# Moving q, k, v preparation beside the first-layer MLP stage and running attention two batches ahead, in a fused attention and MLP kernel

## Chip, cores, metric

One core of one Trainium2 chip. The metric is the device time of one execution in microseconds (us); medians of several runs are quoted, and ratios where two kernels are compared. The trace of one profiled execution per kernel is what the readings rest on; its span lies about 2 us below the time of the same execution.

## The reference, cut to what matters

Batch, heads, sequence and head size are 8, 8, 576 and 64. Model and hidden sizes are 512 and 2048. Inputs and outputs are float32.

```python
scores = scale * q @ k^T + (cum[i] - cum[j])     # cum: running sum of log f
attn   = softmax(causal(scores));  o = attn @ v
x      = o as (B*S, H*D)                          # 4608 tokens of 512
out    = gelu_tanh(x @ w_in) @ w_out              # 512 -> 2048 -> 512
```

## The kernel before

Work goes by groups `i` of four heads, two groups per batch. For one group an *attention step* makes scores (TensorE), exponentials (ScalarE), the causal mask (VectorE), and the product with v for the group before (TensorE). That product carries the row sums along: v is extended by a column of weights. The sums then go through DRAM, for one pair of heads at a time: two small DMAs collect them (`den`), VectorE inverts them, one DMA stores them (`rrow`), two DMAs bring them back broadcast over 64 partitions (`rb`), and POOL multiplies (`scale_out`, writing `xT`, the input of the MLP). I call this the *row-sum chain*.

```python
def step(i, j, old, n, fill, per_round, qk_loads=(), v_loads=()):
    for x in qk_loads: load_qk(x)          # 8 DMAs on the sync queue
    for x in v_loads:  load_v(x)           # 5 DMAs on the sync queue, 256-byte pieces
    for r in range(4):
        if i is not None: score_round(i, r)
        if j is not None: attn_out(j, r); den_load(j, r)
        if r == 0 and n is not None: cast_k(n); cast_q(n)              # POOL
        if r == 1:
            if old is not None: den_spread(old, 1); scale_out(old, 0)  # rrow, rb; POOL
            if n is not None: transpose_k(n)                           # VectorE
        if r == 2:
            if n is not None: transpose_q(n)
            if i is not None: make_vaug(i)                             # POOL
        if i is not None and r > 0: mask(i, r - 1)
        pull(fill, per_round)              # second-layer matmuls fill the gaps
        if r == 3:
            if j is not None: den_spread(j, 0)
            if i is not None: mask(i, 3)
            if old is not None: scale_out(old, 1)                      # last multiply
# ... cut ...
    step(0, None, None, 1, none, 0); step(1, 0, None, None, none, 0)
    for c in range(4): load_w_out(c)       # POOL queue, casts on the way
    step(None, 1, 0, 2, none, 0, qk_loads=[2, 3], v_loads=[2]); finish_out(1)
    for ft in range(N_FT): mlp_in(0, ft)   # first first-layer stage
    fill = mlp_out(out_tiles(0)); pull(fill, 24)
    attention(1, fill, 3); attention(2, fill, 2)
    # ... cut: rest of fill ...
    for ft in range(N_FT): mlp_in(1, ft)   # second first-layer stage
    for b in range(3, B):
        fill = mlp_out(out_tiles(b - 2))
        attention(b, fill, 9)              # two steps, each loading q, k of i+2 and v of i+1
        # ... cut: rest of fill ...
        for ft in range(N_FT): mlp_in(b - 1, ft)
```

`mlp_in(b, ...)` is the *first-layer stage* of a batch, 128 matmuls of 288 columns. It needs all of `xT` of that batch, so only its first six matmuls can run before the last `scale_out`; where it "starts" or "gets going" below is after that wait. The order of instructions is set by hand, and the sync queue issues its DMAs in that order: in the timeline below, a store whose data were ready at 345.4 us is issued at 353.1, after the loads ahead of it.

The softmax here doesn't subtract the row's maximum and nothing guards it: scores larger than these inputs give would overflow.

Of the kernel before, what the change touches and what calls it, by code (L numbers as in the profile page):

```python
# [8 lines left out]
FP32 = mybir.dt.float32  # L9
# [7 lines left out]
def kernel(  # L17
# [10 lines left out]
    nc = tc.nc  # L28
# [32 lines left out]
    singles = ctx.enter_context(tc.tile_pool(name="singles", bufs=1))  # L61
    ostage_pool = ctx.enter_context(tc.tile_pool(name="ostage", bufs=3))
    den_pool = ctx.enter_context(tc.tile_pool(name="den", bufs=3))
    rb_pool = ctx.enter_context(tc.tile_pool(name="rb", bufs=4))
    dram_pool = ctx.enter_context(
        tc.tile_pool(name="scratch", bufs=4, space=bass.MemoryType.DRAM))
    psS = ctx.enter_context(tc.tile_pool(name="psS", bufs=2, space=bass.MemoryType.PSUM))
# [3 lines left out]
    def many(n, shape, dtype, name):  # L71
        return [singles.tile(shape, dtype, name=f"{name}{i}") for i in range(n)]
# [7 lines left out]
    k_nat = many(2, [128, NA, 2, D], FP32, "k_nat")  # L80
    q_bf = singles.tile([128, NA, 2, D], BF16, name="q_bf")
    k_bf = singles.tile([128, NA, 2, D], BF16, name="k_bf")
    v_nat = many(2, [128, NT, 4, D], FP32, "v_nat")
    qT = many(2, [128, S, 2], BF16, "qT")
    kT = many(2, [128, SPAD, 2], BF16, "kT")
    v_aug = many(2, [128, NT, 4, 128], BF16, "v_aug")
# [9 lines left out]
    shift = singles.tile([128, 1], FP32, name="shift")  # L96


    def load_qk(i):
        b, h0 = i // QPB, 4 * (i % QPB)  # L100
        for src, dst in ((k, k_nat[i % 2]), (q, q_nat[i % 2])):

            for h in range(4):
                nc.sync.dma_start(  # L104
                    out=dst[32 * h:32 * h + 32].rearrange("p a e d -> p a (e d)"),
                    in_=src[b, h0 + h].rearrange("(a p e) d -> p a (e d)", p=32, e=2),
                )

    def load_v(i):
        b, h0 = i // QPB, 4 * (i % QPB)  # L110
        for t in range(NT):
            n = min(128, S - 128 * t)
            nc.sync.dma_start(  # L113
                out=v_nat[i % 2][:n, t, :, :],
                in_=v[b, h0:h0 + 4, 128 * t:128 * t + n, :].rearrange("h p d -> p h d"),
            )

    w_in_hbm = moe_w_in.rearrange("(t p) n -> p t n", p=128)
# [22 lines left out]
    def cast_k(i):  # L141
        nc.gpsimd.tensor_copy(k_bf, k_nat[i % 2])

    def cast_q(i):
        nc.gpsimd.tensor_copy(q_bf, q_nat[i % 2])

    def transpose_k(i):
        transpose_one(k_bf, kT[i % 2])

    def transpose_q(i):  # L150
        transpose_one(q_bf, qT[i % 2])

    def make_vaug(i):
        va = v_aug[i % 2].rearrange("p t (x y) c -> p (t x) (y c)", y=2)
        va = va.rearrange("p m (e c) -> p m e c", c=64)
        vn = v_nat[i % 2].rearrange("p t (x y) d -> p (t x) y d", y=2)
        w = wT[:, i, :, :].rearrange("p t (x y) -> p (t x) y", y=2)
        nc.gpsimd.tensor_mul(va[:, :, 0:4:3, :], vn,
                             w.unsqueeze(3).to_broadcast([128, 2 * NT, 2, D]))
        nc.gpsimd.tensor_copy(va[:, :, 1:3, 0:1], w.unsqueeze(3))  # L160

    def score_round(i, r):
# [109 lines left out]
    def out_tiles(b):  # L272
        n0 = 9 * (b // 2)
        return range(n0, n0 + 4) if b % 2 == 0 else range(n0 + 4, n0 + 9)


    def setup():
        nc.sync.dma_start(out=f_sb, in_=f.rearrange("b h s -> (b h) s"))
        for i in range(2):
            load_qk(i)  # L280
            load_v(i)
        make_identity(nc, ident_f32)
        make_upper_triangular(nc, utri_f32, val=1.0, diag=True)
        for t_ in v_nat:
            nc.gpsimd.memset(t_[64:128, NT - 1, :, :], 0.0)
        for t_ in v_aug:
            nc.gpsimd.memset(t_, 0.0)
        cast_k(0)
        cast_q(0)
        for c in range(4):  # L290
            load_w_in(c)

        nc.vector.memset(ones_f32, 1.0)
        nc.vector.memset(wT[64:128, :, NT - 1, :], 0.0)
        nc.vector.memset(shift, -64.0)
        for t_ in kT:
            nc.vector.memset(t_[:, S:SPAD, :], 0.0)
        nc.vector.tensor_scalar(f_sb, f_sb, 1e-4, 1.0, op0=ALU.max, op1=ALU.min)
        nc.scalar.activation(f_sb, f_sb, AF.Ln)
        nc.vector.tensor_copy(utri[:, 0, :], utri_f32)  # L300
        ps_lt = psM.tile([128, NT * BH], FP32, name="ps_lt", tag="m")
        for t in range(NT):
            jw = min(128, S - 128 * t)
            nc.tensor.transpose(ps_lt[:jw, t * BH:(t + 1) * BH],
                                f_sb[:, 128 * t:128 * t + jw], ident_f32)
        nc.vector.tensor_copy(logfT[:, :(NT - 1) * BH], ps_lt[:, :(NT - 1) * BH])
        nc.vector.tensor_copy(logfT[:LAST, (NT - 1) * BH:], ps_lt[:LAST, (NT - 1) * BH:])
        cum_ps = psM.tile([128, NT * BH], FP32, name="cum_ps", tag="m")
        for t in range(NT):
            jw = min(128, S - 128 * t)  # L310
            for tp in range(t + 1):
                jp = min(128, S - 128 * tp)
                lhsT = utri_f32[:jp, :jw] if tp == t else ones_f32[:jp, :jw]
                nc.tensor.matmul(cum_ps[:jw, t * BH:(t + 1) * BH], lhsT,
                                 logfT[:jp, tp * BH:(tp + 1) * BH],
                                 start=(tp == 0), stop=(tp == t))
        for (rows, t0, t1) in ((128, 0, NT - 1), (LAST, NT - 1, NT)):
            nc.scalar.activation(
                wT[:rows, :, t0:t1, :].rearrange("p i t h -> p t i h"),
                cum_ps[:rows, t0 * BH:t1 * BH].rearrange("p (t i h) -> p t i h", i=NQ, h=4),  # L320
                AF.Exp, scale=-1.0, bias=shift[:rows, :])
        transpose_k(0)
        transpose_q(0)


    def pull(it, n):
# [1 line left out]
            if next(it, False) is False:  # L328
                return

    def step(i, j, old, n, fill, per_round, qk_loads=(), v_loads=()):


        for x in qk_loads:
            load_qk(x)
        for x in v_loads:
            load_v(x)
        for r in range(4):
            if i is not None:
                score_round(i, r)  # L340
            if j is not None:
                attn_out(j, r)
                den_load(j, r)
            if r == 0:
                if n is not None:
                    cast_k(n)
                    cast_q(n)
            if r == 1:
                if old is not None:
                    den_spread(old, 1)  # L350
                    scale_out(old, 0)
                if n is not None:
                    transpose_k(n)
            if r == 2:
                if n is not None:
                    transpose_q(n)
                if i is not None:
                    make_vaug(i)
            if i is not None and r > 0:
                mask(i, r - 1)  # L360
            pull(fill, per_round)
            if r == 3:
                if j is not None:
                    den_spread(j, 0)
                if i is not None:
                    mask(i, 3)
                if old is not None:
                    scale_out(old, 1)

    def finish_out(j):  # L370
        den_spread(j, 1)
        scale_out(j, 0)
        scale_out(j, 1)

    none = iter(())

    def attention(b, fill, per_round):
        for i in range(b * QPB, b * QPB + QPB):
            step(i, i - 1 if i > 2 else None, i - 2 if i > 3 else None,
                 i + 1 if i + 1 < NQ else None, fill, per_round,  # L380
                 qk_loads=[i + 2] if i + 2 < NQ else [],
                 v_loads=[i + 1] if i + 1 < NQ else [])

    with tc.manual_schedule():
        setup()
        step(0, None, None, 1, none, 0)
        step(1, 0, None, None, none, 0)
        for c in range(4):
            load_w_out(c)
        step(None, 1, 0, 2, none, 0, qk_loads=[2, 3], v_loads=[2])  # L390
        finish_out(1)
        for ft in range(N_FT):
            mlp_in(0, ft)
        fill = mlp_out(out_tiles(0))
        pull(fill, 24)
        attention(1, fill, 3)
        attention(2, fill, 2)
        for x in fill:
            pass
        for ft in range(N_FT):  # L400
            mlp_in(1, ft)
        for b in range(3, B):
            fill = mlp_out(out_tiles(b - 2))
            attention(b, fill, 9)
            if b == B - 1:
                step(None, NQ - 1, NQ - 2, None, none, 0)
                finish_out(NQ - 1)
            for x in fill:
                pass
            for ft in range(N_FT):  # L410
                mlp_in(b - 1, ft)
        fill = mlp_out(out_tiles(B - 2))
        for ft in range(N_FT):
            mlp_in(B - 1, ft)
            pull(fill, 4)
        for x in fill:
            pass
        for x in mlp_out(out_tiles(B - 1)):
            pass
# [30 lines left out]
```

## Time and profile before

| | before |
|---|---|
| time, median | 485.4 us |
| span of the profiled run | 481.7 us |
| TensorE busy | 366.5 us, 76% |
| first first-layer stage runs without a break from | 76.2 us |
| second first-layer stage starts at | 156.1 us |
| one batch of the steady part (mean of four) | 51.2 us |
| from the seventh first-layer stage to the end | 66.5 us |

The page's first two parts of the kernel before: busy time (PE is TensorE's matmuls, PEld its weight loads, DVE VectorE, ACT ScalarE), and the span in 40 slices of 12 us (busy tenths of TensorE, its granted clock in tenths, that is the share of full clock that the profile records as granted, and the busy tenths of the DMA engines).

```profile
PE 366.5 (76%) x2818; PEld 218.0 (45%) x2851; DVE 147.9 (31%) x253; ACT 204.2 (42%) x274; POOL 182.3 (38%) x148
...
PE   4462107988570999789975999699929997999996
...
PEclk9997556999876999989997999899989999799999
DMA  9969920098955804781286318461643022200111
```

TensorE has the most work, and each notch in its row is idle time. The DMA row stands at 6 to 9 tenths in the first five slices and is high again in spells of every batch later. (This trace has 2818 of the program's 2851 matmuls on record, so its busy time of TensorE is slightly low.)

Stretches of the kernel before, cut where each first-layer stage gets going: length, busy time of PE, PEld, DVE, ACT and POOL, granted clock, DMA share, GB/s. The DMA share adds up the times of the packets and can read above 1.

```profile
0.00:76.17 76.17, 25.56 (x193) 15.58 (x194) 20.52 (x37) 17.72 (x22) 35.73 (x38) 0.78 0.87 159
76.17:156.05 79.88, 55.50 (x463) 30.89 (x469) 27.03 (x49) 38.04 (x50) 31.21 (x24) 0.86 0.58 118
156.05:207.09 51.04, 44.80 (x356) 26.47 (x360) 18.28 (x31) 25.50 (x34) 21.25 (x16) 0.97 0.51 115
207.09:257.77 50.68, 41.55 (x340) 24.97 (x344) 17.41 (x30) 25.52 (x34) 21.27 (x16) 0.94 0.54 121
257.77:308.52 50.75, 45.17 (x357) 26.66 (x360) 18.29 (x31) 25.50 (x34) 21.50 (x16) 0.97 0.49 116
308.52:360.79 52.27, 41.80 (x341) 25.15 (x345) 17.73 (x30) 25.52 (x34) 21.25 (x16) 0.93 0.51 117
```

The first number after the length is TensorE's busy time. A batch takes 51 us for about 43 us of its work. What it waits for, from the view of waits (engine, line, releaser; total us, times, longest):

```profile
PE ps_h L247 <- POOL xT_100 L239: 26.5, 5, 9.2
PE ps_h L247 <- POOL xT_101 L239: 15.8, 3, 11.1
PE ps_h L247 <- POOL xT_102 L239: 13.8, 2, 9.0
```

It is always a multiply of POOL, and in the steady part it is the last one of the batch. The timeline shows why that is late. These are the sync queue's DMA instructions in the second attention step of one batch (start, duration of issue, what), then POOL and TensorE:

```profile
342.38 2.02 SPq L104 DMA_DIRECT2D k_nat_85<-in_k_dram  x4
344.50 2.53 SPq L104 DMA_DIRECT2D q_nat_83<-in_q_dram  x4
347.13 4.55 SPq L113 DMA_DIRECT2D v_nat_88<-in_v_dram  x5
351.77 1.20 SPq L216 DMA_DIRECT2D den<-oT_98  x2
353.07 0.53 SPq L227 DMA_DIRECT2D rrow<-den  x1
354.68 1.12 SPq L230 DMA_DIRECT2D rb<-rrow  x2
```

```profile
357.87 2.86 POOL L239 TENSOR_TENSOR xT_102<-oT_99,rb 64x576 bf16<-64x576 f32 x2 [7.87 <-DMA rb<-rrow]
```

```profile
350.86 0.90 PE L247 MATMUL ps_h<-xT_102,w_in_sb 128*128 128x288 bf16 x6
360.79 0.64 PE L247 MATMUL ps_h<-xT_102,w_in_sb 128*128 128x288 bf16 x2 [9.03 <-POOL xT_102 L239]
```

The inverse was ready at 345.4 us, but its store (`rrow`) was issued at 353.1, behind thirteen loads of k, q and v. The broadcast, the multiply and TensorE follow from there: six first-layer matmuls run, then TensorE idles 9.0 us.

### The profile page before, as it was taken

The page shows a single profiled execution, that of the slowest core. Times are in us where ns is not written, and L with a number is a line of the kernel's source. Part 1 is how long each engine was busy: PE and PEld are TensorE (multiplying, and loading weights), DVE is VectorE, ACT ScalarE, POOL GpSimd, SP SyncE. Part 2 cuts the span into 40 slices and gives each one's busy share as a digit, 9 for nine tenths or more (in the row PEclk, how much of TensorE's full clock was granted, in tenths as well). Part 3 has the DMA queues.
Part 4 walks back from the last instruction along what each step waited for, and adds up shares of the span by engine and source line. Part 5 has one row for each costly group of instructions (what it writes and reads, how often), then busy time and mean ns, then how long its engine had stood idle before and what let it go on. Part 6 is the DMA issues. An engine that isn't in the chain of part 4 may idle for free.

```text
span 481.7 us, 7341 instructions
## 1 busy us (share of the span) xinstructions
PE 366.5 (76%) x2818; PEld 218.0 (45%) x2851; DVE 147.9 (31%) x253; ACT 204.2 (42%) x274; POOL 182.3 (38%) x148
## 2 busy tenths in 40 slices
PE   4462107988570999789975999699929997999996
PEld 4231004734230754356434744374417544676642
DVE  4062200046551026600760066104720267200111
ACT  2551003666440564347442755266425643363310
POOL 8270446014464505480447126530735035620000
PEclk9997556999876999989997999899989999799999
DMA  9969920098955804781286318461643022200111
GB/s 181 212 103 206 219 68 15 1 203 160 172 128 118 174 1 129 160 190 28 75 170 186 58 51 189 146 121 48 148 119 75 1 95 96 73 25 23 44 67 66
DMA packets 95283, 52.32 MB, mean 109 GB/s; under 512 B 45520, under 2 KB 86480, under 8 KB 95248
## 3 DMA queue, kind: packets, MB, share of 16 engines
q1 hardware_dynamic: 91024, 47.65, 43.6%
q0 software_dynamic: 4224, 4.19, 5.3%
q8 instruction: 22, 0.36, 0.3%
q14 instruction: 13, 0.11, 0.1%
HBM read 46.28 MB, written 9.58 MB: 116 GB/s over the span
## 4 chain that ended last, share of the span: by engine, by line
PE 49%; DMA 12%; SPq 7%; issue 3%; DVE 3%; POOL 3%; ACT 1%; DVEq 0%; POOLq 0%; ACTq 0%
PE ps_h L247 24%; PE pso L264 16%; PE po L200 6%; DMA rrow<-den 4%; PE ps_s L171 3%; SPq L104 3%; DMA v_nat_88<-in_v_dram 2%; DMA rb<-rrow 2%; SPq L113 2%; SPq L230 1%; POOL xT_101 L239 1%; DMA den<-oT_98 1%; DMA k_nat_85<-in_k_dram 1%; POOL xT_102 L239 1%; DMA den<-oT_99 1%
## 5 line engine op out<-in xcount | busy, mean ns | idle before, releaser
L254 ACT ACTIVATE gT<-ps_h 128x576 bf16<-128x576 f32 x128 | 83.4, 651 | 156.5 <-PE ps_h L247 156.5
L247 PEld LDWEIGHTS <-w_in_sb 128*128 128x128 bf16 x1024 | 104.4, 102 | 93.0 <-issue 59.0
L264 PE MATMUL pso<-w_out_sb,gT 128*128 128x512 bf16 x543 | 132.1, 383 | 2.1 <-issue 0.6
L264 PEld LDWEIGHTS <-gT 128*128 128x128 bf16 x576 | 52.9, 99 | 57.3 <-issue 6.2
L180 ACT ACTIVATE pt_97<-ps_s 128x800 bf16<-128x800 f32 (+3 forms) x64 | 50.1, 834 | 56.4 <-PE ps_s L171 47.5
L247 PE MATMUL ps_h<-xT_100,w_in_sb 128*128 128x288 bf16 x384 | 52.6, 301 | 26.5 <-POOL xT_100 L239 26.5
L207 DVE COPY oT_99<-po 128x576 f32<-128x576 f32 x32 | 24.2, 755 | 147.5 <-PE po L200 147.4
L247 PE MATMUL ps_h<-xT_101,w_in_sb 128*128 128x288 bf16 x384 | 53.5, 297 | 15.8 <-POOL xT_101 L239 15.8
L180 ACT ACTIVATE pt_96<-ps_s 128x800 bf16<-128x800 f32 (+3 forms) x64 | 50.1, 834 | 32.9 <-PE ps_s L171 23.8
L268 DVE COPY o_st<-pso 128x512 f32<-128x512 f32 x36 | 24.5, 680 | 87.1 <-PE pso L264 87.1
L200 PE MATMUL po<-pt_97,v_aug_95 128*128 128x320 bf16 (+4 forms) x224 | 29.9, 274 | 21.4 <-DVE oT_99 L207 17.4
L247 PE MATMUL ps_h<-xT_102,w_in_sb 128*128 128x288 bf16 x256 | 34.8, 301 | 13.8 <-POOL xT_102 L239 13.8
L200 PE MATMUL po<-pt_96,v_aug_94 128*128 128x320 bf16 (+4 forms) x224 | 31.1, 279 | 11.5 <-DVE pt_96 L189 6.0
L239 POOL TENSOR_TENSOR xT_100<-oT_98,rb 64x576 bf16<-64x576 f32 x12 | 16.9, 1412 | 47.4 <-DMA rb<-rrow 47.0
L200 PEld LDWEIGHTS <-v_aug_95 128*128 128x128 bf16 x224 | 19.3, 101 | 33.5 <-issue 28.0
L207 DVE COPY oT_98<-po 128x576 f32<-128x576 f32 x32 | 24.2, 756 | 27.7 <-PE po L200 27.4
L239 POOL TENSOR_TENSOR xT_101<-oT_98,rb 64x576 bf16<-64x576 f32 x12 | 17.0, 1413 | 40.8 <-DMA rb<-rrow 39.2
L200 PEld LDWEIGHTS <-v_aug_94 128*128 128x128 bf16 x224 | 19.2, 103 | 23.0 <-issue 12.4
L171 PE MATMUL ps_s<-qT_90,kT_92 32*128 32x400 bf16 (+5 forms) x384 | 23.3, 295 | 7.2 <-ACT pt_96 L180 4.7
L239 POOL TENSOR_TENSOR xT_102<-oT_98,rb 64x576 bf16<-64x576 f32 x8 | 11.3, 1418 | 40.4 <-DMA rb<-rrow 40.0
L171 PE MATMUL ps_s<-qT_91,kT_93 32*128 32x400 bf16 (+5 forms) x384 | 20.6, 300 | 6.3 <-DVE qT_91 L134 4.6
L189 DVE TENSOR_TENSOR pt_96<-pt_96,utri 128x512 bf16<-128x512 bf16 (+1 forms) x40 | 22.9, 591 | 5.4 <-ACT pt_96 L180 5.4
(54 smaller groups left out, 255.2 us busy)
## 6 DMA issues: line engine op xcount, KB each, us to landing
rb<-rrow SPq DMA_DIRECT2D x64, 144.0 KB, 3.1
out_dram<-o_st SPq DMA_DIRECT2D x36, 256.0 KB, 2.2
k_nat_84<-in_k_dram SPq DMA_DIRECT2D x32, 144.0 KB, 3.6
q_nat_82<-in_q_dram SPq DMA_DIRECT2D x32, 144.0 KB, 4.3
k_nat_85<-in_k_dram SPq DMA_DIRECT2D x32, 144.0 KB, 3.7
q_nat_83<-in_q_dram SPq DMA_DIRECT2D x32, 144.0 KB, 4.6
v_nat_88<-in_v_dram SPq DMA_DIRECT2D x32, 128.0 KB, 4.7
v_nat_89<-in_v_dram SPq DMA_DIRECT2D x32, 128.0 KB, 4.6
```

What stands on the lines that cost most here:

```text
L104: nc.sync.dma_start(out=dst[32 * h:32 * h + 32].rearrange("p a e d -> p a (e d)"), in_=src[b, h0 + h].rearrange("(a p e) d -> p a (e d)", ...
L113: nc.sync.dma_start(out=v_nat[i % 2][:n, t, :, :], in_=v[b, h0:h0 + 4, 128 * t:128 * t + n, :].rearrange("h p d -> p h d"),)
L171: nc.tensor.matmul(tiles[h // 2][:, h % 2, c0:c0 + nq], kk[32 * h:32 * h + 32, 128 * t:128 * t + 128, c], qq[32 * h:32 * h + 32, q0:q0 + n ...
L180: nc.scalar.activation(p[:, 2 * g:2 * g + 2, off:off + n], tiles[g][:, :, 0:n], AF.Exp, scale=scale)
L189: nc.vector.tensor_mul(p[:, :, o:o + w], p[:, :, o:o + w], utri[:, :, :w].to_broadcast([128, 4, w]))
L200: nc.tensor.matmul(po[:, base + s - a:base + z - a], va[:, t, h, :], p[:, h, strip_off[t] + s - 128 * t:strip_off[t] + z - 128 * t], start ...
L207: nc.vector.tensor_copy(oT[i % 2][:, h, :], po[:, 256:256 + S])
L239: nc.gpsimd.tensor_mul(xT[b % 3][s, 2 * u + x, :], oT[i % 2][s, 2 * x + y, :], rb[s, :])
L247: nc.tensor.matmul(ph[:, j, 0:hS], w_in_sb[:, dt, 128 * ft:128 * ft + 128], xT[b % 3][:, dt, hS * j:hS * (j + 1)], start=(dt == 0), stop=( ...
L254: nc.scalar.activation(gT[:, ft, o:o + S].rearrange("p (j n) -> p j n", j=2), ph[:, :, 0:hS], AF.Gelu_apprx_tanh)
L264: nc.tensor.matmul(pso, gT[:, ft, c:c + 128], w_out_sb[:, ft, :], start=(ft == 0), stop=(ft == N_FT - 1))
L268: nc.vector.tensor_copy(st, pso)
```

## The change

The intent is to clear the row-sum chain of traffic. Casts, transposes and all loads of a batch go to the first-layer stage, where POOL, VectorE and the sync queue have little to do. v is loaded once per batch instead of once per group. At the start, attention of batches 0 and 1 runs before the first first-layer stage, so that the loop has one form throughout. Six second-layer matmuls are held over into the next first-layer stage. The first two loads of q are issued from ScalarE's queue. Three smaller edits that follow from these are not shown: v's product with its weights is made in two multiplies, there are three `rb` buffers instead of four, and the first cast of q is VectorE's.

```diff
-    v_nat = many(2, [128, NT, 4, D], FP32, "v_nat")
+    v_nat = many(2, [128, NT, H, D], FP32, "v_nat")
...
+    def prepare(b):
+        for i in range(b * QPB, b * QPB + QPB):
+            cast_k(i); transpose_k(i); cast_q(i); transpose_q(i)
+            if i + QPB < NQ:
+                load_qk(i + QPB)
+        if b + 1 < B:
+            load_v(b + 1)
...
         setup()
-        # (start as above)
+        step(0, None, None, none, 0, n=1)
+        load_qk(2); load_v(1)
+        step(1, 0, None, none, 0, n=2)
+        load_qk(3); load_qk(4)
+        step(2, 1, 0, none, 0, n=3)
         for c in range(4):
             load_w_out(c)
+        load_qk(5)
+        step(3, 2, 1, none, 0)
+        load_v(2)
+        fill = none
+        for b in range(2, B + 1):
+            for ft in range(N_FT):
+                mlp_in(b - 2, ft)
+                if ft == 1:
+                    for x in fill: pass            # the six held over
+                    if b < B: prepare(b)
+            fill = mlp_out(out_tiles(b - 2))
+            if b < B:
+                held = 64 + 16 * (b % 2) - 6
+                for i in range(b * QPB, b * QPB + QPB):
+                    step(i, i - 1, i - 2, fill, held // 8)
...                                                # (tail as before)
```

(Statements joined on a line for brevity; cuts marked by "...".)

More of the change, by code (lines that the diff above doesn't have):

```diff
@@ L63 @@
     den_pool = ctx.enter_context(tc.tile_pool(name="den", bufs=3))
-    rb_pool = ctx.enter_context(tc.tile_pool(name="rb", bufs=4))
+    rb_pool = ctx.enter_context(tc.tile_pool(name="rb", bufs=3))
     dram_pool = ctx.enter_context(
@@ L96, with load_heads, load_v @@
     shift = singles.tile([128, 1], FP32, name="shift")
-    def load_qk(i):
-        b, h0 = i // QPB, 4 * (i % QPB)
-        for src, dst in ((k, k_nat[i % 2]), (q, q_nat[i % 2])):
-            for h in range(4):
-                nc.sync.dma_start(
-                    out=dst[32 * h:32 * h + 32].rearrange("p a e d -> p a (e d)"),
-                    in_=src[b, h0 + h].rearrange("(a p e) d -> p a (e d)", p=32, e=2),
-                )
-    def load_v(i):
-        b, h0 = i // QPB, 4 * (i % QPB)
+    def load_heads(src, dst, i, eng):
+        b, h0 = i // QPB, 4 * (i % QPB)
+        for h in range(4):
+            eng.dma_start(
+                out=dst[i % 2][32 * h:32 * h + 32].rearrange("p a e d -> p a (e d)"),
+                in_=src[b, h0 + h].rearrange("(a p e) d -> p a (e d)", p=32, e=2),
+            )
+    def load_qk(i):
+        load_heads(k, k_nat, i, nc.sync)
+        load_heads(q, q_nat, i, nc.sync)
+    def load_v(b):
         for t in range(NT):
@@ L113, in load_v @@
             nc.sync.dma_start(
-                out=v_nat[i % 2][:n, t, :, :],
-                in_=v[b, h0:h0 + 4, 128 * t:128 * t + n, :].rearrange("h p d -> p h d"),
+                out=v_nat[b % 2][:n, t, :, :],
+                in_=v[b, :, 128 * t:128 * t + n, :].rearrange("h p d -> p h d"),
             )
@@ L155, in make_vaug @@
         va = va.rearrange("p m (e c) -> p m e c", c=64)
-        vn = v_nat[i % 2].rearrange("p t (x y) d -> p (t x) y d", y=2)
         w = wT[:, i, :, :].rearrange("p t (x y) -> p (t x) y", y=2)
-        nc.gpsimd.tensor_mul(va[:, :, 0:4:3, :], vn,
-                             w.unsqueeze(3).to_broadcast([128, 2 * NT, 2, D]))
+        for x in range(2):
+            hx = 4 * (i % QPB) + 2 * x
+            nc.gpsimd.tensor_mul(
+                va[:, x:2 * NT:2, 0:4:3, :], v_nat[(i // QPB) % 2][:, :, hx:hx + 2, :],
+                w[:, x:2 * NT:2, :].unsqueeze(3).to_broadcast([128, NT, 2, D]))
         nc.gpsimd.tensor_copy(va[:, :, 1:3, 0:1], w.unsqueeze(3))
@@ L279, in setup @@
         for i in range(2):
-            load_qk(i)
-            load_v(i)
+            load_heads(k, k_nat, i, nc.sync)
+            load_heads(q, q_nat, i, nc.scalar)
+            if i == 0:
+                load_v(0)
         make_identity(nc, ident_f32)
@@ L285, in setup @@
             nc.gpsimd.memset(t_[64:128, NT - 1, :, :], 0.0)
+        cast_k(0)
         for t_ in v_aug:
             nc.gpsimd.memset(t_, 0.0)
-        cast_k(0)
-        cast_q(0)
         for c in range(4):
@@ L321, in setup @@
                 AF.Exp, scale=-1.0, bias=shift[:rows, :])
+        nc.vector.tensor_copy(q_bf, q_nat[0])
+        transpose_q(0)
         transpose_k(0)
-        transpose_q(0)
     def pull(it, n):
@@ L329, in pull, with step @@
                 return
-    def step(i, j, old, n, fill, per_round, qk_loads=(), v_loads=()):
-        for x in qk_loads:
-            load_qk(x)
-        for x in v_loads:
-            load_v(x)
+    def step(i, j, old, fill, per_round, n=None):
         for r in range(4):
@@ L343, in step @@
                 den_load(j, r)
-            if r == 0:
-                if n is not None:
-                    cast_k(n)
-                    cast_q(n)
+            if r == 0 and n is not None:
+                cast_k(n)
+                cast_q(n)
             if r == 1:
@@ L375 @@
     none = iter(())
-    def attention(b, fill, per_round):
+    def prepare(b):
         for i in range(b * QPB, b * QPB + QPB):
-            step(i, i - 1 if i > 2 else None, i - 2 if i > 3 else None,
-                 i + 1 if i + 1 < NQ else None, fill, per_round,
-                 qk_loads=[i + 2] if i + 2 < NQ else [],
-                 v_loads=[i + 1] if i + 1 < NQ else [])
+            cast_k(i)
+            transpose_k(i)
+            cast_q(i)
+            transpose_q(i)
+            if i + QPB < NQ:
+                load_qk(i + QPB)
+        if b + 1 < B:
+            load_v(b + 1)
@@ L384 @@
     with tc.manual_schedule():
         setup()
-        step(0, None, None, 1, none, 0)
-        step(1, 0, None, None, none, 0)
+        step(0, None, None, none, 0, n=1)
+        load_qk(2)
+        load_v(1)
+        step(1, 0, None, none, 0, n=2)
+        load_qk(3)
+        load_qk(4)
+        step(2, 1, 0, none, 0, n=3)
         for c in range(4):
             load_w_out(c)
-        step(None, 1, 0, 2, none, 0, qk_loads=[2, 3], v_loads=[2])
-        finish_out(1)
-        for ft in range(N_FT):
-            mlp_in(0, ft)
@@ L394 @@
-        fill = mlp_out(out_tiles(0))
-        pull(fill, 24)
-        attention(1, fill, 3)
-        attention(2, fill, 2)
-        for x in fill:
-            pass
-        for ft in range(N_FT):
-            mlp_in(1, ft)
-        for b in range(3, B):
-            fill = mlp_out(out_tiles(b - 2))
-            attention(b, fill, 9)
-            if b == B - 1:
-                step(None, NQ - 1, NQ - 2, None, none, 0)
-                finish_out(NQ - 1)
-            for x in fill:
-                pass
-            for ft in range(N_FT):
-                mlp_in(b - 1, ft)
@@ L412 @@
-        fill = mlp_out(out_tiles(B - 2))
+        load_qk(5)
[6 more added lines that the diff above has]
+                if ft == 1:
+                    for x in fill:
+                        pass
+                    if b < B:
+                        prepare(b)
+            fill = mlp_out(out_tiles(b - 2))
+            if b < B:
+                held = 64 + 16 * (b % 2) - 6
+                for i in range(b * QPB, b * QPB + QPB):
+                    step(i, i - 1, i - 2, fill, held // 8)
+                if b == B - 1:
+                    step(None, NQ - 1, NQ - 2, none, 0)
+                    finish_out(NQ - 1)
+                pull(fill, held % 8)
```

## The prediction

> **What bounds it now.** TensorE's own work, with holes. The busy table gives PE 366.5 us of 481.7 (76%). Stretches cut at each start of a first-layer MLP stage show one batch of the steady part taking 51.0, 50.7, 50.8 and 52.3 us for 44.8, 41.6, 45.2 and 41.8 us of PE work. The waits say what PE waits for: its first-layer matmuls want the last scaled attention rows (xT, POOL): 56 us in all, 4.1, 7.7 and 9.0 us in the three stretches from 257 us. The chain of waits shows what is behind it: sum rows go to DRAM and back as a broadcast (median landings 1.8 and 3.1 us), but those DMAs stand in the sync queue behind the step's q, k and v loads (k 2.0, q 2.5, v 4.6 us of issue time, between a reciprocal at 345.1 us and its store at 353.1 us). The last multiply then starts at 357.9 us, long after PE ran out. Second, the start: the second first-layer stage begins only at 156 us. From 76 to 156 us PE works 55.5 us at a mean granted clock of 0.86; before 76 us the DMA share is 0.87.
>
> **What the change does.** PE keeps its instructions, in another order at the start. Casts (1.17 us each, POOL), transposes (0.75 us, DVE) and q, k, v loads go to the beginning of the 16.7 us first-layer stage, where POOL and DVE idle; four casts with transposes between should take about 8 us: hidden. v costs 40 instead of 80 DMA issues but the same 256-byte pieces, so its engine time hardly falls; the Trainium skill, "DMA: Bandwidth & Descriptors", Specifications, gives 512 B as least size for line rate, and the profile has 45,520 of 95,283 packets under it. A batch's 3.5 MB at about 200 GB/s (what full slices moved) takes an estimated 18 us: it just fits beside the first-layer stage, clear of the row-sum traffic.
>
> **Steady part.** Unblocked, a reciprocal 6 us into a step lets rows land at 12 us and the last multiply end at 15 us, against steps of 12.2 to 13.8 us: 1 to 3 us of wait stay per batch. Estimated periods are 45 and 47.5 us, and 53.5 us for the last with its final attention step: five periods 238.5 us against 259 us, about 21 us saved.
>
> **Start.** Attention of batches 0 and 1 now runs before the first first-layer stage. Its loads (about 13 MB with both weights) are DMA-bound, and group 3's k waits behind the first row-sum chain in the sync queue. I expect that stage's steady start at 75 us (76 before), with two attention steps more behind it. The second stage then starts near 121 us instead of 156: 35 us saved, the larger and less certain term.
>
> **Tail** from the seventh first-layer stage: 66.5 us, unchanged.
>
> Sum: 75 + 45.5 + 238.5 + 66.5 = 425.5 us of span; times lie 2 to 3 us above: 428 us, range 416 to 444. Chances: faster 0.96, within 2% 0.03, slower 0.01.
>
> **What would show it.** Waits of first-layer matmuls on xT fall from 56 to under 25 us, below 3.5 us each in the steady part; q, k, v loads lie within 23 us of a stage's start; PE stays near 360 us busy, its share about 85%, clock about 0.95.
>
> **What would make it wrong.** The start may stall more: a whole batch's v delays the next k and q, or the second weight load (issued only after a scaling multiply) collides with group 5's loads; each could add 10 us. If loads outlast the first-layer stage they again hold up row sums, and 5 us a period return. If the waits vanish wholly, 416 us is possible.

## The result, and the profile after

The changed kernel takes 434.2 us (429.8 to 435.7, four runs) against 485.4 us; the ratio is 0.894, 95% interval 0.888 to 0.900. Ratios here are the mean time of one kernel's runs over that of the other's in the same rounds, so not quite the ratio of the medians quoted. Executions over 1.5% slower than the fastest of the same kernel are left out of the means. The profiled run took 433.2 us with a span of 431.4.

The page's first two parts, after (slices of 10.8 us):

```profile
PE 359.9 (83%) x2851; PEld 215.7 (50%) x2851; DVE 165.9 (38%) x254; ACT 204.0 (47%) x274; POOL 183.9 (43%) x163
...
PEclk9997858559999999999999999999999996999999
DMA  9997939779622962298229732983200222201011
```

From the eleventh slice on the clock is 9 tenths or more in every slice but one, where it was broken before. The DMA row now has a sharp rhythm: 8 or 9 tenths beside each first-layer stage, 2 or 3 in the attention steps. VectorE's busy time rose from 147.9 to 165.9 us; 15 of these 18 us are the same 80 masks taking longer (588 ns before, 780 after, on average). TensorE waited no longer for them than before; why they are slower was not looked into.

The same stretches, after:

```profile
0.00:90.44 90.44, 37.63 (x317) 21.57 (x318) 33.42 (x55) 30.24 (x38) 43.73 (x47) 0.78 0.89 168
90.44:135.65 45.21, 41.66 (x339) 24.98 (x339) 20.12 (x29) 25.49 (x34) 21.64 (x18) 0.94 0.69 149
135.65:178.72 43.07, 42.62 (x355) 25.30 (x355) 18.11 (x28) 25.49 (x34) 20.47 (x18) 1.00 0.59 136
178.72:222.49 43.77, 41.23 (x352) 25.02 (x351) 22.13 (x33) 25.49 (x34) 22.43 (x19) 1.00 0.61 140
222.49:265.76 43.27, 42.77 (x354) 25.31 (x354) 19.46 (x30) 25.50 (x34) 20.72 (x18) 1.00 0.61 136
265.76:310.59 44.83, 41.29 (x351) 25.01 (x350) 22.45 (x34) 25.50 (x34) 22.43 (x19) 1.00 0.57 137
```

A steady batch takes 43.7 us on average instead of 51.2 (I call these four stretches the *inner periods*). The second first-layer stage starts at 135.7 us instead of 156.1. But the first one gets going only at 90.4 us. The waits after:

```profile
PE ps_h L251 <- POOL xT_100 L243: 22.1, 3, 20.1
PE ps_h L251 <- POOL xT_101 L243: 1.9, 1, 1.9
PE ps_h L251 <- POOL xT_102 L243: 1.8, 1, 1.8
```

One single wait of 20.1 us, at the start, is most of what is left of these waits. In the steady part the row-sum chain runs freely; the sync queue, POOL and TensorE in the second step of a batch:

```profile
214.84 0.52 SPq L231 DMA_DIRECT2D rrow<-den  x1
216.42 1.12 SPq L234 DMA_DIRECT2D rb<-rrow  x2
```

```profile
219.49 2.94 POOL L243 TENSOR_TENSOR xT_100<-oT_99,rb 64x576 bf16<-64x576 f32 x2 [0.30 <-DMA rb<-rrow]
```

```profile
220.65 0.90 PE L251 MATMUL ps_h<-xT_100,w_in_sb 128*128 128x288 bf16 x6
222.49 1.39 PE L251 MATMUL ps_h<-xT_100,w_in_sb 128*128 128x288 bf16 x10 [0.94 <-POOL xT_100 L243]
```

From the store's issue to the end of the multiply it takes 7.6 us, about as before (353.1 to 360.7); what is gone is the delay ahead of the store. Compare the bracket: 0.94 us of waiting instead of 9.03.

The start's wait is read from the chain of waits of the changed kernel (start, duration, what). `k_nat_85` is group 5's load of k, `rrow` the store of group 1's last row sums:

```profile
65.15 9.63 DMA k_nat_85<-in_k_dram
...
74.85 9.63 DMA rrow<-den
...
84.53 2.87 DMA rb<-rrow
...
87.53 1.40 POOL xT_100 L243
...
90.44 17.59 PE ps_h L251 x122
```

The store was issued only once that load had landed. In the trace, the sync queue's DMAs use eight completion semaphores in turn, and a DMA waits until the earlier one with its semaphore has landed; for this store that was the third of the four loads of group 5's k. Then the store itself, 4.5 KB, took 9.6 us to land, while w_out (issued at 63.8 us, landed by 83.6) and group 5's q (landed by 84.0) were under way. The median for such a store was 1.8 us before.

So the terms of the whole difference, 481.7 − 431.4 = 50.3 us of span: the start up to the second first-layer stage gave 20.4, the five periods to the seventh stage 259.2 − 226.4 = 32.7, and the tail took back 2.8.

### The profile page after: what moved, and what is told of

The parts are those of the page before. It is cut to its first block, busy times and chain, and to the rows that moved or that the text cites. A ratio compares the mean times of both kernels' runs of the same rounds, so it can differ in the third digit from the quotient of the medians.

```text
span 431.4 us, 7325 instructions
## 1 busy us (share of the span) xinstructions
PE 359.9 (83%) x2851; PEld 215.7 (50%) x2851; DVE 165.9 (38%) x254; ACT 204.0 (47%) x274; POOL 183.9 (43%) x163
## 4 chain that ended last, share of the span: by engine, by line
PE 66%; DMA 16%; SPq 6%; DVE 5%; POOL 3%; issue 2%; ACT 1%; DVEq 0%; POOLq 0%
PE ps_h L251 30%; PE pso L268 24%; PE po L204 8%; PE ps_s L175 4%; DMA rrow<-den 4%; SPq L103 4%; DMA q_nat_82<-in_q_dram 3%; DVE pt_96 L193 3%; DMA k_nat_84<-in_k_dram 3%; DMA k_nat_85<-in_k_dram 2%; DMA rb<-rrow 2%; POOL xT_100 L243 1%; SPq L115 1%; ACT gT L258 1%; DMA den<-oT_99 1%
## 5 line engine op out<-in xcount | busy, mean ns | idle before, releaser
L268 PE MATMUL pso<-w_out_sb,gT 128*128 128x512 bf16 x576 | 136.4, 380 | 0.0
L251 PEld LDWEIGHTS <-w_in_sb 128*128 128x128 bf16 x1024 | 101.8, 99 | 60.1 <-issue 27.7
L251 PE MATMUL ps_h<-xT_100,w_in_sb 128*128 128x288 bf16 x384 | 52.3, 300 | 22.2 <-POOL xT_100 L243 22.1
L251 PE MATMUL ps_h<-xT_101,w_in_sb 128*128 128x288 bf16 x384 | 50.5, 286 | 1.9 <-POOL xT_101 L243 1.9
L272 DVE COPY o_st<-pso 128x512 f32<-128x512 f32 x36 | 24.7, 687 | 69.6 <-PE pso L268 69.5
L204 PE MATMUL po<-pt_97,v_aug_95 128*128 128x320 bf16 (+4 forms) x224 | 30.4, 279 | 10.6 <-DVE oT_99 L211 8.1
L204 PE MATMUL po<-pt_96,v_aug_94 128*128 128x320 bf16 (+4 forms) x224 | 31.7, 282 | 8.6 <-POOL v_aug_94 L164 4.6
L193 DVE TENSOR_TENSOR pt_97<-pt_97,utri 128x512 bf16<-128x512 bf16 (+1 forms) x40 | 35.6, 904 | 0.0
L251 PE MATMUL ps_h<-xT_102,w_in_sb 128*128 128x288 bf16 x256 | 32.3, 286 | 1.9 <-POOL xT_102 L243 1.8
L243 POOL TENSOR_TENSOR xT_101<-oT_98,rb 64x576 bf16<-64x576 f32 x12 | 17.0, 1421 | 38.2 <-DMA rb<-rrow 37.7
L243 POOL TENSOR_TENSOR xT_100<-oT_98,rb 64x576 bf16<-64x576 f32 x12 | 17.0, 1419 | 32.1 <-DMA rb<-rrow 31.6
L175 PE MATMUL ps_s<-qT_90,kT_92 32*128 32x400 bf16 (+5 forms) x384 | 23.1, 303 | 9.0 <-ACT pt_96 L184 3.4
L243 POOL TENSOR_TENSOR xT_100<-oT_99,rb 64x576 bf16<-64x576 f32 x12 | 17.1, 1428 | 23.7 <-DMA rb<-rrow 23.2
L193 DVE TENSOR_TENSOR pt_96<-pt_96,utri 128x512 bf16<-128x512 bf16 (+1 forms) x40 | 25.7, 662 | 0.0
```

What stands on the lines that cost most here:

```text
L175: nc.tensor.matmul(tiles[h // 2][:, h % 2, c0:c0 + nq], kk[32 * h:32 * h + 32, 128 * t:128 * t + 128, c], qq[32 * h:32 * h + 32, q0:q0 + n ...
L193: nc.vector.tensor_mul(p[:, :, o:o + w], p[:, :, o:o + w], utri[:, :, :w].to_broadcast([128, 4, w]))
L204: nc.tensor.matmul(po[:, base + s - a:base + z - a], va[:, t, h, :], p[:, h, strip_off[t] + s - 128 * t:strip_off[t] + z - 128 * t], start ...
L243: nc.gpsimd.tensor_mul(xT[b % 3][s, 2 * u + x, :], oT[i % 2][s, 2 * x + y, :], rb[s, :])
L251: nc.tensor.matmul(ph[:, j, 0:hS], w_in_sb[:, dt, 128 * ft:128 * ft + 128], xT[b % 3][:, dt, hS * j:hS * (j + 1)], start=(dt == 0), stop=( ...
L268: nc.tensor.matmul(pso, gT[:, ft, c:c + 128], w_out_sb[:, ft, :], start=(ft == 0), stop=(ft == N_FT - 1))
```

## Experiments

All kernels gave correct results. In the expectations, times without a name are the changed kernel's.

### Which moved part makes the steady gain?

Two theories. **L**: the loads ahead of the row-sum DMAs in the sync queue. **P**: casts on POOL and transposes on VectorE between the steps' own work.

**Loads back into the steps, casts stay.**

```diff
 def prepare(b):            # casts, transposes only
-            if i + QPB < NQ: load_qk(i + QPB)
-        if b + 1 < B: load_v(b + 1)
...
+                    if i + QPB < NQ:
+                        load_qk(i + QPB); load_v_half(i + QPB)
                     step(i, i - 1, i - 2, fill, held // 8)
```

> Changed kernel, but q, k and half-batch v loads go back to the head of each attention step (as before); casts and transposes stay beside the first-layer stage. Theory L (loads ahead of the row-sum DMAs in the sync queue caused the waits of the kernel before): the last scaling multiply of a batch comes 3 to 6 us later, waits of first-layer matmuls on xT of 3 to 8 us return in each steady period, and the mean of the four inner periods (43.7 us changed, 51.2 us before) rises to 48 to 51 us; time 455 to 470. Theory P (casts on POOL and transposes on DVE inside the steps caused them): periods stay within 1.5 us of 43.7, time within 8 us of 434.

Measured: 476.0 to 481.1 us in three runs, ratio to before 0.988 (0.982 to 0.994). Nearly the whole gain is gone, more than either theory's range. The profiled execution of this kernel fell into another state altogether (1246.6 us of span, first-layer matmuls of 742 ns on average, against 286 to 300 in the changed kernel), so its inner waits are not read; only the timed runs count. This run has the six held-over matmuls and the new order of the loop as well, so these alone do not make the gain.

**Casts and transposes back into the steps**, most loads stay. For lack of memory for a third q and k buffer, the second group's q and k had to be loaded in the first step.

```diff
-            cast_k(i); transpose_k(i); cast_q(i); transpose_q(i)
-            if i + QPB < NQ:
+            if i + QPB < NQ and i % 2 == 0:
                 load_qk(i + QPB)
...                                     # in step(), r == 0
                 cast_k(n); cast_q(n)
+                if n % 2 == 1 and n > 4 and n + QPB < NQ:
+                    load_qk(n + QPB)
...                                     # transposes at r == 1 and 2, n = i + 1
```

> Changed kernel, but casts and transposes go back into the attention steps (as before), while the v load and the q, k load of the first group stay beside the first-layer stage; q, k of the second group are loaded in the first step, once their buffers are cast. Theory L: the inner periods stay within 2 us of 43.7 us, time 434 to 445. Theory P: periods rise to 48 to 51 us, time 455 to 470. The seven transposes per step cost DVE 1.5 us and may bring back the 0.8 us waits of attention products on the mask.

Measured: 451.3 us (445.6 to 453.0). Two of the four runs, the profiled one among them, count as slow; the ratio of the fast ones to before is 0.924. The inner periods are 48.2 us. The period lies in theory P's range, the time in neither's, and two things were mixed in the run. The next run separates them. (The "seven transposes" of the expectation are two per step.)

**Only that one load in the first step**, at the same place in the queue; casts and transposes as in the changed kernel.

```diff
-            if i + QPB < NQ:
+            if i + QPB < NQ and i % 2 == 0:
                 load_qk(i + QPB)
...                                     # in step(), r == 0
+            if r == 0 and late is not None:
+                load_qk(late)          # late = i + 3 in the first step of a batch
```

> Changed kernel, but the second group's q and k load is left in the first attention step, at the very place in the sync queue where the run with casts in the steps had it; casts and transposes stay beside the first-layer stage. It separates the two things that run mixed (451 us, inner periods 48.2 us). Theory L (its loss came from that load): 447 to 453, periods 47.5 to 48.5. Theory P (its loss came from casts and transposes in the steps): 433 to 437, periods near 43.7. In between: both have a share, to be read from the periods.

Measured: 452.6 us (451.3 to 453.6), ratio 0.933; inner periods 48.0 us. One q and k load of 1.2 MB per batch costs as much as the mixed run did, so casts and transposes inside the steps add nothing that shows to what this load costs. Its sync queue, in the first step of a batch:

```profile
256.97 1.89 SPq L103 DMA_DIRECT2D q_nat<-in_q_dram  x4
259.60 0.53 SPq L231 DMA_DIRECT2D rrow<-den  x1
```

The inverse for this store was ready at 257.5 us, 2.1 us before its issue; at the same place of an earlier batch of the changed kernel it was 0.4 us (202.0 and 202.4). Theory L stands, and P is not needed. But no run has casts in the steps with all loads out of them, so that the casts alone would cost nothing is not shown. In the changed kernel POOL idles 3.5 us before the first multiply of a second step (at 213.3 us), and two casts take 2.3 us; from this I estimate that the casts, at least, would fit.

TensorE's waits in the two runs, with casts in the steps and then with the load alone:

```profile
232.18 2.56 PE L251 MATMUL ps_h<-xT,w_in_sb 128*128 128x288 bf16 x10 [4.21 <-POOL xT L243]
281.62 2.15 PE L251 MATMUL ps_h<-xT,w_in_sb 128*128 128x288 bf16 x10 [2.77 <-POOL xT L243]
```

```profile
232.22 2.56 PE L251 MATMUL ps_h<-xT,w_in_sb 128*128 128x288 bf16 x10 [4.12 <-POOL xT L243]
281.88 2.56 PE L251 MATMUL ps_h<-xT,w_in_sb 128*128 128x288 bf16 x10 [3.14 <-POOL xT L243]
```

The lines answer to the one of the changed kernel with 0.94 in its bracket. The wait also makes the ten matmuls after it slower, 2.56 us instead of 1.39: the granted clock reads 0.50 from 232.2 to 234.8 us, and 1.00 at the same place of the changed kernel. The Trainium skill, "TensorE: Matmul & The Clock Gate", Part 1, has the clock halved after an idle window of about 3.4 us; the trace agrees where the wait was 4 us (2.56 / 1.39 = 1.84), and shows the slow matmuls after 3.1 us as well.

**Both back: only the new start is left.**

> Changed kernel with both back in the attention steps: only the new order of the start, attention two batches ahead, is left. Both theories: inner periods 50 to 52 us as before, five periods about 255 us instead of 226; the start keeps its gain of about 20 us against the kernel before; time 460 to 470. If the time is below 445, the steady gain came from the order of the second-layer products held over, not from the moved work.

The edit joins the first two: no preparation beside the first-layer stage, loads at the head of each step, casts and transposes inside it. Measured: 476.2 us (473.9 to 478.7), ratio 0.983, inner periods 52.5 us. TensorE again:

```profile
193.43 2.56 PE L260 MATMUL ps_h<-xT,w_in_sb 128*128 128x288 bf16 x10 [6.55 <-POOL xT L252]
```

The long waits are back (5.6 to 7.3 us at each of the five stages). This is the same within noise as loads back alone (476 to 481): once the loads block the chain, the casts do not matter. I expected 460 to 470. The new start gives the second first-layer stage at 139.9 us, 16 us earlier than before, but the steady part is 1.3 us per batch slower than in the kernel before, so 7.1 us of span are left of it (474.6 against 481.7). That the steady gain is gone while the held-over matmuls stay also settles the rival that the expectation names, the order of those matmuls.

### v once per batch

```diff
-            load_v(b + 1)                       # 5 DMAs
+            load_v_half(QPB * (b + 1))          # 5 DMAs of four heads each
+            load_v_half(QPB * (b + 1) + 1)
```

> Changed kernel, but each batch of v is loaded as two halves of four heads (10 DMAs of 128 and 64 KB instead of 5 twice as large, same bytes and 256-byte pieces). Theory F (v once per batch is a matter of issue count only, and the loads lie beside the first-layer stage anyway): time within 1% of 434. Theory G (fewer, larger DMAs feed the engines better): loads outlast the stage by 2 us or more, row sums wait, 438 or more.

Measured: 435.1 us, ratio to before 0.897 (the changed kernel: 0.894); inner periods 44.3 us. Theory F holds: within this run's resolution the larger loads give nothing by themselves.

### Where does the start's wait of 20.1 us come from?

Theories **A** (w_out's bytes), **B** (group 5's loads ahead in the queue), **C** (both).

```diff
# w_out late
-        for c in range(4): load_w_out(c)
         load_qk(5)
...
+                    if b == 2:
+                        for c in range(4): load_w_out(c)
                     if b < B: prepare(b)
# group 5 late
-        load_qk(5)
         step(3, 2, 1, none, 0)
+        load_qk(5)
```

w_out late:

> Changed kernel, but the second weight load (w_out, 2.1 MB written) is issued at the start of the first first-layer stage instead of before the last start-up step. Theory A (w_out's bytes delay the row-sum DMAs of group 1, whose store took 9.6 us to land): the stage's 20.1 us wait falls to about 10 us, steady start near 80 us instead of 90.4, time 424 us. Theory B (only the k and q loads of group 5, which stand before that store in the sync queue, delay it): wait stays above 17 us, time within 2 us of 434. Theory C (both share the DMA engines): half of the wait goes, as in A, and the rest only with both moved. Risk: w_out lands too late for the second-layer products at about 17 us into the stage; then a new wait there.

Group 5 late:

> Changed kernel, but k and q of group 5 are loaded after the last start-up step instead of before it. Theory A (w_out's bytes): the 20.1 us wait stays above 15 us, time 432 to 435. Theory B (queue position behind group 5's loads): wait falls to about 5 us, time near 419. Theory C (both): wait falls by about half, time near 424.

Both late:

> Both moved. All theories: the row-sum chain of group 1 is clear (store lands in about 2 us, broadcast in 3 us, multiply ends near 75 us), wait at most 6 us, time near 419. If A or B alone was right, one of the other two runs equals this one. If still above 428, the cause is none of these loads.

Measured: 432.6, 429.3 and 433.9 us (ratios 0.893, 0.886 and 0.895). All three missed the 424, 424 and 419 us of theory C, and by the third expectation's own rule (above 428, none of these loads is the cause) the times would clear the loads. The traces do not: the wait itself behaved as theory C has it. The 20.1 us fell to 9.6, 11.0 and 5.4, and the first-layer stage got going at 79.3, 81.3 and 74.8 us instead of 90.4. Yet the time hardly followed. TensorE's waits with both late:

```profile
74.77 17.49 PE L251 MATMUL ps_h<-xT,w_in_sb 128*128 128x288 bf16 x122 [5.40 <-POOL xT L243]
116.05 0.64 PE L204 MATMUL po<-pt,v_aug 128*128 128x320 bf16 x3 [10.80 <-DVE pt L193]
132.49 1.39 PE L251 MATMUL ps_h<-xT,w_in_sb 128*128 128x288 bf16 x10 [2.92 <-POOL xT L243]
```

VectorE in the same run:

```profile
115.35 0.37 DVE L229 RECIPROCAL den<-den 32x36 f32<-32x36 f32 x1 [11.50 <-DMA den<-oT]
115.64 0.55 DVE L193 TENSOR_TENSOR pt<-pt,utri 128x512 bf16<-128x512 bf16 x2
```

A new wait of 10.8 us stands one stage later. The loads of batches 2 and 3 now run into the attention steps; the sums' DMA is issued at 111.7 us, behind v, the reciprocal waits for it, and the masks behind the reciprocal hold up TensorE. With w_out late it is 7.6 us. The gain of 15.7 us at the first stage is down to 3.2 us at the second (132.5 against 135.7). Group 5 late alone keeps 7.1 us (128.6).

### Is the start bound by bytes or by order?

Stretches of the changed kernel in the start (DMA share and GB/s are the last two columns):

```profile
0.00:54.00 54.00, 28.68 (x235) 16.75 (x235) 21.57 (x37) 22.70 (x29) 23.48 (x29) 0.91 1.03 192
54.00:65.00 11.00, 5.42 (x47) 2.50 (x47) 6.72 (x10) 3.02 (x4) 9.96 (x10) 0.51 0.38 85
65.00:90.00 25.00, 3.53 (x37) 2.32 (x37) 5.13 (x10) 4.52 (x5) 9.90 (x10) 0.63 0.80 150
90.00:112.00 22.00, 21.10 (x160) 14.69 (x159) 3.87 (x5) 13.25 (x19) 10.28 (x10) 0.87 1.08 205
```

The engines are full except between 54 and 90 us. Three runs try to use that.

q on the sync queue again, since ScalarE's first activation came 4.3 us later than in the kernel before, after its own DMA issues:

> Changed kernel, with the first two q loads on the sync queue as before instead of the scalar engine's queue. The trace shows ScalarE's first activation start at 9.3 us instead of 4.95, after its own DMA issues, and the first scores at 17.4 instead of 13.2 us. Theory D (that 4 us reaches the end): time falls by about 4 us, to 430. Theory E (the start is bound by DMA bytes, so a late first step is absorbed): first scores again near 13 us, but the first first-layer stage's start and the time stay within 2 us.

Measured: 434.8 us (one of the four runs counts as slow; ratio of the fast ones 0.896); the first scores are at 14.3 instead of 17.4 us, and the first first-layer stage gets going at 90.6. Theory E's forecast holds: the late first step is absorbed. The Trainium skill, "DMA: Bandwidth & Descriptors", Issuing engines are not separate DMA queues, says that issuing from several engines only saves issue time. This pair of runs agrees: issuing from two queues instead of one saved none of the total.

w_out one step earlier, then the same with group 5 late:

> Changed kernel with w_out issued one step earlier, before the third start-up step, so that it fills the stretch from 54 to 65 us where the DMA engines are 3 tenths busy. Theory H (the start is bound by the DMA engines' total work, and moving a load only moves the wait, unless it fills an idle stretch): group 3's k and q land up to 5 us later, but the 20 us wait of the first first-layer stage shrinks to about 10 us; the second stage starts 4 to 8 us earlier than 135.7; time 426 to 431. Rival (only the position in the sync queue matters, DMA bytes are not scarce): wait unchanged, time 434 or more, since group 3 is only delayed.

> w_out early as in the other run and group 5's k and q after the last start-up step (which alone gave 429.3). Theory H: w_out in the idle stretch, the row sums of group 1 clear of all large loads, wait under 5 us; the loads of batches 2 and 3 end before 106 us instead of 112; time 422 to 427. Rival: no better than 429.

Measured: 433.7 and 431.4 us. The idle stretch is filled (with both edits the DMA share from 54 to 65 us is 1.21), but TensorE then waits 15.2 us in the third step, while POOL waits 16.1 us to cast group 3's k, and the share from 65 to 90 us falls to 0.49: the idle stretch has moved. Theory H expected 426 to 431 and 422 to 427, so both times missed their range, by 2.7 and 4.4 us. The wait of the first stage did shrink to 10.2 us in the first run, but the second stage came only 1.0 us earlier.

Group 3's q and k ahead of v and of the first row-sum chain, with group 5 late:

```diff
-        load_qk(2); load_v(1)
+        load_qk(2); load_qk(3); load_v(1)
         step(1, 0, None, none, 0, n=2)
-        load_qk(3); load_qk(4)
+        load_qk(4)
...                                     # and load_qk(5) after step(3, ...)
```

> A version that should beat both kernels: group 5's k and q after the last start-up step (429.3 alone), and group 3's k and q straight after group 2's, ahead of the second batch of v and of the first row-sum chain, behind which they waited in the sync queue until 44 us. Theory H (DMA-bound start with idle stretches made by the sync queue's order): group 3's casts at about 40 us instead of 50 to 53, the third and fourth steps 8 to 12 us earlier, first first-layer stage steady near 72 us, second near 121; time 418 to 424. Rival (the start is bound by bytes alone): 427 to 430.

Measured: 429.1 us (426.1 to 431.4), ratio 0.885. The casts of group 3 did come at 40 to 42 us instead of 50 to 53, but the first multiply now waited for its row sums until 51.4 us (they were behind v), w_out was issued at 64.6 (63.8 in the changed kernel), and the second stage starts at 129.4. So theory H (418 to 424) missed and the time lies in the rival's range (427 to 430, bytes alone), but this run does not prove the rival, since it equals group 5 late alone (ratio 0.886), and so does the run with w_out early and group 5 late (0.886). These three beat the changed kernel by about 1%, with intervals that touch (0.881 to 0.890 for group 5 late against 0.888 to 0.900), on different chips: a likely small gain, not a settled one. Over the first 112 us the mean DMA share is 0.93 in the changed kernel and 0.93 to 0.99 in the five variants where it was read, so the engines were busy for most of the start in every order. Whether bytes or order set the start, and what would bring it near its floor, stays open; in every variant the waits moved rather than went.

## Why the prediction was right or wrong

The time, 434.2 us, lies in the range (416 to 444) and 6 us above the 428 predicted. The sum hides two terms that were off by more, in opposite directions; that they nearly cancelled is luck.

| term | predicted | measured (profiled run) |
|---|---|---|
| first first-layer stage gets going | 75 | 90.4 |
| from there to the second | 45.5 | 45.2 |
| five periods to the seventh | 238.5 | 226.4 |
| tail | 66.5 | 69.3 |
| span | 425.5 | 431.4 |

- **The mechanism of the steady part was right.** That loads ahead of the row-sum DMAs in the sync queue made the waits is shown: loads back alone lose nearly the whole gain, one load back alone costs 4.3 us a batch, and casts and transposes add nothing to that. The loads lie beside the first-layer stage as predicted: in the stage from 178.7 us they are issued from 183.5 to 199.2, inside the 23 us predicted. The four casts took 6.4 us there, 7.2 with the last transpose (estimate: 8).
- **Its size was too small: about 33 us came, not 21.** The predicted "1 to 3 us of wait" per batch was 0 to 1.9 us (mean 0.9). And the work itself shrank: TensorE's busy time in an inner period fell from 43.3 to 42.0 us at an unchanged instruction list (up to the six matmuls that move between periods, and the few that the first trace lacks), while the granted clock went from 0.95 to 1.00. I had taken the work from periods in which part of it ran at the lower clock after each wait. The experiment with 4 us waits shows that cost directly, 2.56 against 1.39 us.
- **The step that failed is "that stage's steady start at 75 us".** It came at 90.4, so the start saved 20 us and not 35. The store of group 1's row sums waited for group 5's k and then took 9.6 us beside w_out. The prediction named this collision among its risks at 10 us; it belonged in the sum. By 90 us the DMA engines had moved 168 GB/s × 90.4 us = 15 MB, more than the 13 MB estimated. The experiments show both loads share the delay (9.6 and 11.0 us left with one moved, 5.4 with both). But they also show that mending it gains little: 15.7 us earlier at the first stage are 3.2 us at the second.
- **The tail was 2.8 us longer.** Of this, 1.5 us are the six held-over matmuls that now stand in it, and most of the rest is the stage's first sixteen matmuls, which took 3.6 us; twice eight took 2.3 us at full clock (1.14 each). The granted clock is 0.92 in that stretch, against 1.00 before. The gaps of the last attention products stand just ahead of it, but that they are the cause was not tested.
- **"Its engine time hardly falls" for v was right:** by the traces' packet records, the 256-byte packets of v took 56.8 us of the 16 engines' time before and 53.6 after, and loading v as halves again changes nothing that shows. No run changes the size of the pieces. In the trace before, 256-byte packets took 24.7 ns each, the 512-byte ones of q and k 39.4 ns, and the 2048-byte ones of the output's stores 87.5 ns: of these three the smallest moved the fewest bytes per ns (10.4), in line with the skill's 512 bytes, but the 512-byte loads also moved fewer than the 2048-byte stores (13.0 against 23.4).
- Waits on xT were to fall under 25 us: 25.8 us, of which 20.1 is the one at the start. TensorE's share was to be about 85% and the clock 0.95: 83% and 0.94.

## What to carry to other kernels

Look at what stands ahead of a small, latency-bound DMA in its queue; moving bulk loads into a stage where no such chain runs was worth most of the 33 us of the steady part here, and a wait taken away also gave back the slow matmuls after it. In the start, where the DMA engines were busy most of the time (mean share 0.93 over the first 112 us), moving one load moved the wait: follow the gain to the next stage before counting it. A total that comes out right says little; check each term, here one was 15 us too low and another 12 us too high.

## What the Trainium skill lacked or had wrong

- "DMA: Bandwidth & Descriptors", Bandwidth: its table has 341 GB/s for 1 MB loads issued from POOL. With this kernel's mix, mostly 256-byte and 512-byte pieces on the sync queue, the 16 engines were full (share 1.03 and 1.08) at 192 and 205 GB/s (in the first of these stretches w_in's loads from POOL are among them). The page has no rate for such a mix on that queue.
- "DMA: Bandwidth & Descriptors", Latency and other measured facts: it gives about 2 us as a DMA's fixed cost. The median 4.5 KB store agreed (1.8 us), but one took 9.6 us among large loads, landing just after them; the page gives no landing time for a small DMA queued in such company.
- "TensorE: Matmul & The Clock Gate", Part 1: the idle window of about 3.4 us is said to run freely, but what a shorter wait costs the page does not give in numbers. In these runs ten matmuls took 1.39 us after every wait of up to 1.9 us. Above that it varied: 2.48 us after a wait of 2.05 us and 2.15 after 2.8, but 1.39 after 2.2 and after 2.9; after 4 us or more it was 2.3 to 2.6 us.
- "TensorE: Matmul & The Clock Gate", Part 1: one profiled execution had matmuls of 742 ns instead of about 300 throughout and a span of 1246.6 us, with a granted clock recorded as 1.0; the same kernel's three other runs took 476 to 481 us. Only TensorE was slow in it (ScalarE's gelu took 650 ns on average, as in the kernel before). The page tells of a clock stuck at a quarter for over 50 us and warns that the trace's clock events can be wrong, but not of a whole execution that is slow while the record calls it unthrottled.
